# Row variances of layer norm moved from VectorE to GpSimd, with a rebuilt instruction order

## The chip, the cores and the metric

One core of one Trainium2 chip in each run. The metric is the device time of one execution in microseconds (us). All runs quoted here are in the fast state (granted TensorE clock 0.99 to 1.00), apart from one run of the kernel before that came in the slow state and is left out of every ratio.

## The reference, cut to what matters

Four residual layers over 2048 tokens of 512 values, alternating a linear attention (A) and a dilated local attention (B). A layer norm without learned parameters stands before each:

```python
def _layernorm(x, axis=-1, eps=1e-5):
    m = jnp.mean(x, axis=axis, keepdims=True)
    v = jnp.var(x, axis=axis, keepdims=True)
    return (x - m) / jnp.sqrt(v + eps)

x = A_x
x = x + _A_ref(_layernorm(x), A_wqkv, A_w_phi, A_wo)
x = x + _B_ref(_layernorm(x), B_wqkv, B_wo)
x = x + _A_ref(_layernorm(x), A_wqkv, A_w_phi, A_wo)
x = x + _B_ref(_layernorm(x), B_wqkv, B_wo)
# ... (the two attentions: softmax feature maps with running sums; 8 keys at distance 2)
```

## The kernel before

The tokens are worked on in four blocks of 512 (128 rows by 4 columns of row statistics). Three of the four norms get their statistics from the layer that comes before: the residual add leaves the row sums, a square on ScalarE leaves the sums of squares, and a small step `var` makes the variance from both. That is 3 norms x 4 blocks = 12 variances.

```python
def sq(t):                                   # ScalarE, four per block
    sqd = self.t2([D], "sqd")
    nc.scalar.activation(out=sqd[:], in_=xb[:, t, :], func=ACT.Square, accum_out=T["ss"][:, t:t + 1])

def var(lo, n):                              # VectorE: q = ss - u*u/D
    u = T["sums"][:, lo:lo + n]
    nc.vector.scalar_tensor_tensor(out=T["q"][:, lo:lo + n], in0=u, scalar=-1.0 / D, in1=u,
                                   op0=ALU.mult, op1=ALU.mult)
    nc.vector.tensor_tensor(out=T["q"][:, lo:lo + n], in0=T["q"][:, lo:lo + n],
                            in1=T["ss"][:, lo:lo + n], op=ALU.add)
# ... s_norm:
def ln():                                    # ScalarE: "the logarithm"
    nc.scalar.activation(out=U["lnv"][:, 0:n], in_=T["var"](), func=ACT.Ln, bias=self.eps_t[:, 0:1], scale=scale)
    nc.scalar.activation(out=U["rstd"][:, 0:n], in_=U["lnv"][:, 0:n], func=ACT.Exp, scale=-0.5)
def nmr():                                   # VectorE: -mean * rstd
    # ...
```

The program is a set of threads of steps. A list of thread numbers says in which order the steps are emitted, a string says which of two engines does each copy, and another string says which numbered buffer each new tile gets:

```python
for w in _ORDER.split():
    key = self.names[int(w, 36)]
    i = n.get(key, 0); n[key] = i + 1
    self.threads[key][i]()
# ...
def slot(self, kind):
    k = self.ntile[kind]; self.ntile[kind] = k + 1
    return kind + _SLOTS[kind][k]
```

Each engine works through its own instructions in emission order, so one that has to wait for another engine's result holds up the work behind it in the list.

Of the kernel before, what the change touches and what calls it, by code (L numbers as in the profile page):

```python
# [8 lines left out]
BF16 = mybir.dt.bfloat16  # L9
# [7 lines left out]
P = 128  # L17
# [24 lines left out]
    "half_k": ((0, 3), (1, 3)),  # L42
    "half_ln": (),
    "split": ((1, 2), (1, 3)),
    "v_dram": (),
    "half_mo": (),
    "rho_pad": 0,
# [10 lines left out]
av 8 i i i i i i i i i i i i 0 f 0 g e 2t 0 bs 9 h a d c 0 j k t i i j l 27 o p 3 3 d6 b 1x 1x t 1y o m 2 2 1q  # L58
1z 1x 1x q u t r 1q v x w n s 1r w 1s 4 20 y 21 1x 22 1x 23 1q 1q 1q 1q 1v 1w z 3d 3d 3d 1u 1t 25 3e 3e 3e z 5
3e 3e z z 26 10 18 18 d5 1 z 16 11 4i 15 6 1h 13 3d 3e 3e 25 25 26 18 25 18 12 26 26 28 26 26 26 26 19 12 28  # L60
2a 28 1h 18 14 12 12 1a 28 1c 3e 2g 2g 1f 2h 2h 1h 1h 1b 1i 2b 1b 1e 1d 29 2j 2k 1h 1j 1n 2r 1b 1l 2s 1b 2c 2r
1k 2s 17 2g 2g 2h 2h 1k 1k 2h 2h 2h 2h 2d 1g 2d 2d 2d 2e 2j 1m 35 36 32 2o 2o 33 2s 33 32 33 33 2r 2s 2s 1o 2o
2o 2d 2r 3a 1k 3a 1p 2p 2o 24 24 2s 24 2u 2v 35 37 2u 2u 2u 2s 2i 2w 2j 3a 2s 3a 2l 2z 2j 24 32 32 34 2m 3b 33
3d 3f 3f 2z 2z 2z 33 2f 33 33 2f 2f 2f 3a 3a 2q 2q 2q 30 3a 2n 3a 3a 2z 3e 2q 2x 35 35 b6 3b 3a 2y 31 31 31 31
3c 3c 38 3c 39 3c 3m 3f 3n 3o 3o 3o 24 24 3g 3g 3g 3f 3p 3q 3g 3g 3g 3g 3g 3r 3q 3f 3g 24 3h 3i 3i 5l 5m 5n 3p
3s 3q 3j 3k 3k 3t 3q 3p 3x 5m 3w 3u 3h 3i 3i 3q 3v 3q 3q 3y 3h 3i 3q 3i 3h 3i 3q 5l 5o 5p 5r 5m 5q 7 7 3z 3q
3i 3j 3k 5m 5l 5s 3k 7 7 5m 5m 5m 3h 3i 7g 40 5u 44 41 42 5t 5m 5m 3j 3j 7h 7i 3k 5v 5m 5w 43 7h 45 7j 45 60
3k 3k 3k 46 45 45 5y 5x 5z 61 61 48 47 47 61 49 47 4a 47 4b 62 47 4b 63 3j 4g 94 4c 45 4d 45 4e 4f 3k 45 45 61
64 63 4h 4p 65 95 7j 7j 66 4q 63 96 95 97 97 63 67 7h 63 67 69 7h 6b 4k 4k 4k 4l 4p 4r 4k 4m 4p 4p 4s 4t 7k 7n
6a 68 6c 4o 7m 50 50 4u 4u 4u 4n 4u 7l 4w 97 7o 7p 7p 7q 7s 3l 4x 7r 7r 7p 7t 7p 6o 7u 50 7r 7r 7v 6o 6j 4v 4y  # L70
4j 6o 6q 6o 4j 4z 6k 6p 6r 6j 7r 6e 6l 95 6d 95 7v 6t 6s 6f 6d 7w 6e 7z 7x 98 9b 9a 99 6g 7y 9c 6e 6j 6j 9d 9d
6u 9d 6e 6n 80 6m 9d 6h 6v 6v 9e 9h 9f 6i 9g 9f 6w 6v 6v 6w 6w 9f 9i 9f 87 88 8h 9j 9f 50 82 9j 9l 6w 6x 6x 87
87 6w 81 83 9n 6x 9k 87 8b 89 51 51 51 51 52 52 8c 8c 8e 6u 6u 6u 9m 8j 8a 8d 8c 6v 6y 3l 8f 82 9o 82 85 82 50
51 52 4z 4z 4z 9q 9q 9s 8c 6z 8g 6y 6z 9r 71 70 6y 6y 6z 6z 72 86 a0 a0 a1 73 84 8i 74 75 74 74 50 74 8i 76 8i
77 a2 76 79 53 53 54 55 54 a5 56 53 54 9v 78 76 9q 9q 76 a0 81 53 9v 9w 9p 7a 57 9v 9u a7 76 7a 9t 8j 7c 9y 54
58 59 59 59 9v 59 9x 7d 7e 5a 8j 8j 7b 7f 5c 5b 5d 5b 5b a0 8k 5e 5b 5f 8k 9z a7 5b 5f 5j 8k 8k 8l a3 5i b4 a4
b7 5h b4 b4 b4 8l 5g b5 b5 a7 b5 b5 a7 8k 8l 8j c3 8i c3 b8 c4 c4 c4 c4 a8 8m a8 a8 a8 c3 a9 a9 5k at c1 b5 a6
8m au au c1 c2 b5 c2 aw c2 c2 a8 a9 b5 b5 8n 8o 8n 8p 8m at au at at 8n 8q 8m a7 aa 8n aw 8r 8s au au au 8s 8s
8t au au 8s 8v a6 a6 8u aa 8w aa 8x 8u 8u 8u 8y ab ac ab ad a6 aa b7 8u b9 b7 c3 8y 90 92 c1 91 c1 c2 8z c2 c2
aw ay ab c2 ba ae ab af aw b0 c4 c4 b1 bc ag ag ag ag ah bc aj ak bc c1 c4 c4 bc al ax c3 ai ai ai bd b1 ai am  # L80
93 bf bi bg az bf ai am ar bf bf bg bg aq b7 bg bg bg bg bg bb an ao ag ag ap bi ag ag b1 b1 bc b2 c2 bi bn bi
bl bk as bq br br bq br br bq bq b1 br by by by by bt b3 b3 b3 b3 br be be be br br bz c5 c5 bh bj bn bn bn c5
bu c4 by by by by c6 bo by c6 c6 c5 bt bt bt bn bv c6 c6 c6 bz be bp bp bw bm bp bp c0 c0 by c6 c6 bx c0 c0 c9
c5 ca c6 cb cb cc cb cd ce cd fr fs c7 c8 c7 c8 c8 ft cc ci cf cd cg cd c7 c8 c8 fs fu c8 e2 fu ch cd e3 cd cc
cj ck e4 cd c7 c8 c8 c7 e3 e2 cm cd c8 e6 e7 fu cl cd cd cn cp co e5 e3 hb e3 cr e2 ea e9 cq hc cs e3 cs e8 e3
e3 hd eb ec e3 e3 e3 ed ct cv hc eh cs he ee cs ef cw eg ei cx ei ei cu ei cu cu cu fs cy fs fv ej cu cy d0 cz
ek d2 fw fx fz d3 cs cs fy cs cs g0 g0 g0 el ek em ek en ek d4 d1 dc g1 eo ek g2 g3 g2 dc de eo es g0 g4 dd dh
g2 g5 g2 he hc eq g6 d7 d8 d7 d7 d7 he di dc g2 dc d9 ep er hc et dn hf da db df dh dh dh hi hh hj hg hk hk hk
dj dk dl dm dm g6 g7 g9 dn dn dg ga f0 f0 hl hm hn hm ho hm ev ew f1 hk dn g8 do do hp f2 fa fc hm hq do do dp
ev ex fc gb ev f0 dp ey dn f3 f0 hm fc f4 hq ev ez fc do dp dn dq dq d6 f5 f6 dm dm eu hs gi gj gi fd gs hr fd  # L90
ht fd hu hv fd dq fe fe f5 f5 f8 f5 f9 f7 fb gk fd fe fc gn gn gp gi gi gl gm gd gd gd ge ic gf i7 i7 i9 gg i8
dr dr dt ds dr du hx hy gd dq gu dr dv gn gq gh i7 ff ia gu fb go ff fg fh fb fb eu gv gc gn i2 gr i3 hx hz hx
i7 i2 ib gv i4 hx i1 gc hw i2 i2 i5 gu i0 gu gv gv gw gt ie fg fi if i6 ie id gw if dw dx id gv gw id id ie ie
if if ig dw ff ig if ig fg fj dw e0 dw ff fg fk ie fl fm fl fn gu fl fl fp ih ih ih ih e1 ii ii ii ik ij fq dy
gt gt gt fo fo il io io io io ii im ip iq ip is ir ir ih ii in ip ip iu it ir gx ir gy gx gx gx gz gy h0 dz dz
iv gy h1 h4 gx gy h2 h4 iw iv h5 h5 h6 h7 gy h4 h3 h5 h8 h9 h7 h7 h4 h5 ha h7
# [4 lines left out]
    "0011111111111001110111111010000010010000000000000001011111101100100000110101000110000010000001110111"  # L101
    "1101011110010000110101000000000000001101011000000000100100000000000000000101111100000011011000000000"
    "0000000000001101111010000000100101011111010000011001110111000000000000000111111011101110010100101000"
    "00000000000001111001000000000000000000000000000000000000000000000000000000000001111"
# [5 lines left out]
        "0123456701231231456204632073205712053720457604356704213560421356720415763215063506432506"  # L110
    ),
    "med": (
        "0123456789abcdef5837ae98eeaeae471853bc9e43cbe47199ce3185413cebf94c8f74e3581bc71931bc7f370bf9ac21584e"
        "af9c37214a0b589dec37"
    ),
    "t2": (
        "0123450123450342150132451032451032451032451302153421530421503452014520345123045130425123504321504321"
        "5043215043210451023134"
    ),
    "ps": (  # L120
        "0123456701234750613250746132074365462150743510635127035164051362731405263710452763210743562107423251"
        "0764376215043762435107625407152367423167052341760543210675432170652147053624036542076314257603415203"
        "6415026734107534105234065265346053460562036207346201542015471204712603712035764120356471032516407324"
        "6735012463754021637261350247613025476130746513072463501742635017463015276301562703152760432764327014"
        "6570324650324705613245076"
# [4 lines left out]
class _Fast:  # L130
# [162 lines left out]
    def setup(self):  # L293
# [12 lines left out]
        self.VD = {}  # L306
# [202 lines left out]
    def s_out(self, st, key, b, Wo, last):  # L509
# [36 lines left out]
        def var(lo, n):  # L546
            if "q" not in T:
                T["q"] = self.sm([4], "q")
            u = T["sums"][:, lo:lo + n]
            nc.vector.scalar_tensor_tensor(out=T["q"][:, lo:lo + n], in0=u, scalar=-1.0 / D, in1=u,  # L550
                                           op0=ALU.mult, op1=ALU.mult)
            nc.vector.tensor_tensor(out=T["q"][:, lo:lo + n], in0=T["q"][:, lo:lo + n],
                                    in1=T["ss"][:, lo:lo + n], op=ALU.add)

        def norm(lo, n):
            add(st, "DVE", var, lo, n)
            V = {"var": lambda: T["q"][:, lo:lo + n], "sum": lambda: T["sums"][:, lo:lo + n]}
            self.s_norm(st, key, b, V, tuple(range(lo, lo + n)), 1.0 / D, 1.0 / D)
# [24 lines left out]
    def s_a1(self, L, b):  # L583
# [3 lines left out]
        G = 2 * H  # L587

# [48 lines left out]
        def t1(t, m):  # L637
            T["s1"] = self.sm([4 * G], "s1", F32, 1)
            nc.vector.tensor_tensor(out=T["s1"][:, 0:m * G], in0=T["s2"][:, 0:m * G, 0], in1=T["s2"][:, 0:m * G, 1],
                                    op=ALU.add)  # L640
# [36 lines left out]
        for t in range(4):  # L677
            add(st + "v", "PE", mv, t)
            self.flex(st + "v", ev, t)
        m = 2 if (L, b) in _OPT["half_k"] else 4  # L680
        for t in range(0, 4, m):
            for f in (t8, t4, t2, t1):
                add(st, "DVE", f, t, m)
# [235 lines left out]
    def s_b1(self, L, b):  # L919
# [83 lines left out]
        if (L, b) in _OPT["v_dram"]:  # L1003
            add(st + "v", "SP", vwr)
# [813 lines left out]
```

## Time and profile before

| | before |
|---|---|
| median, lowest to highest of the first runs | 330.5 us, 329.39 to 330.88 |
| span of the profiled run | 327.5 us |
| TensorE, VectorE, ScalarE, GpSimd busy | 310.3, 302.2, 279.3, 25.3 us |
| ScalarE's waits for the variance before the logarithm | 1.9 us in 7 waits |

The busy rows are sums over stages with different limits.

### The profile page before, as it was taken

The numbers are of one execution on the slowest core, as the hardware profiler recorded it, in microseconds if no ns is written. First come the engines' busy times: TensorE is split into PE (matmuls) and PEld (weight loads), VectorE is DVE, ScalarE is ACT, GpSimd is POOL, SyncE is SP. The second block draws the span as 40 slices with busy tenths as digits, with TensorE's granted clock in tenths as the row PEclk, the third lists the DMA queues.
The fourth block names the chain that finished last, engine by engine and source line by source line (L and its number), as shares of the span: only waits on it lengthen the run. The fifth ranks groups of instructions, "written<-read, shape, count | busy, mean of one in ns | idle before, by whom it ended". The sixth has DMA issues, their size and how long they took to land. (4 is left out here: it accounts for less than half of the span.)

```text
span 327.5 us, 8033 instructions
## 1 busy us (share of the span) xinstructions
PE 310.3 (95%) x3176; PEld 149.5 (46%) x3203; DVE 302.2 (92%) x439; ACT 279.3 (85%) x634; POOL 25.3 (8%) x50
## 2 busy tenths in 40 slices
PE   7999999999999999999999999979999999999873
PEld 3655456445444444443444455644544454433221
DVE  7998995998998999899999999699999999999993
ACT  5999988998888999989999999798999996676550
POOL 4000000000021003000000000000000208400000
PEclk9999999999999999999999999999999999999999
DMA  7980000004556899998750300023436977679952
GB/s 197 380 197 3 0 2 4 2 20 120 105 148 135 152 164 133 139 121 154 137 135 1 67 3 2 4 59 90 128 58 125 179 146 134 150 139 158 166 176 92
DMA packets 37388, 35.41 MB, mean 108 GB/s; under 512 B 23008, under 2 KB 32224, under 8 KB 37344
## 3 DMA queue, kind: packets, MB, share of 16 engines
q1 hardware_dynamic: 36816, 34.81, 53.6%
q8 instruction: 27, 0.44, 0.6%
q14 instruction: 17, 0.14, 0.2%
q10 hardware_dynamic: 528, 0.02, 0.1%
HBM read 10.50 MB, written 2.36 MB: 39 GB/s over the span
## 5 line engine op out<-in xcount | busy, mean ns | idle before, releaser
L927 PE MATMUL ps<-xnT,WB 128*128 128x512 bf16 x384 | 87.6, 380 | 0.5 <-DMA xnT<-xn 0.5
L1081 DVE TENSOR_TENSOR pav<-PT,Vg 128x4096 bf16<-128x4096 bf16 (+1 forms) x34 | 72.0, 2162 | 1.5 <-DMA Vg<-V 1.0
L1019 DVE TENSOR_TENSOR prod<-QT,K 128x4096 bf16<-128x4096 bf16 x32 | 72.5, 2291 | 0.3 <-ACT QT L192 0.2
L927 PEld LDWEIGHTS <-WB 128*128 128x128 bf16 x384 | 42.3, 114 | 43.3 <-issue 5.8
L520 PEld LDWEIGHTS <-oT 128*128 128x128 bf16 x256 | 23.8, 97 | 34.5 <-ACT oT L192 5.7
L192 ACT CAST oT<-ps 128x512 bf16<-128x512 f32 (+1 forms) x60 | 32.1, 587 | 8.4 <-PE ps L1090 7.1
L706 ACT ACTIVATE Eq<-ps 128x512 bf16<-128x512 f32 x64 | 34.0, 615 | 0.7 <-PE ps L698 0.6
L520 PE MATMUL ps<-WoB,oT 128*128 128x512 bf16 x122 | 32.1, 380 | 2.4 <-ACT oT L192 2.0
L599 ACT ACTIVATE Ek<-ps 128x512 bf16<-128x512 f32 x64 | 33.6, 622 | 0.4 <-PE ps L593 0.2
L698 PE MATMUL ps<-xnT,WA 128*128 128x512 bf16 x128 | 30.7, 380 | 0.6 <-DVE Eq L816 0.6
L540 ACT ACTIVATE sqd<-x 128x512 bf16<-128x512 bf16 x48 | 30.1, 643 | 1.0 <-DVE x L533 0.8
L605 PE MATMUL ps<-WA,xnT 128*128 128x512 bf16 x120 | 30.0, 380 | 0.5 <-issue 0.2
L593 PE MATMUL ps<-WA,xnT 128*128 128x512 bf16 x124 | 29.7, 380 | 0.6 <-DMA xnT<-xn 0.2
L520 PE MATMUL ps<-WoA,oT 128*128 128x512 bf16 x120 | 29.2, 380 | 0.4
L533 DVE SCALAR_TENSOR_TENSOR x<-ps,x 128x512 bf16<-128x512 f32 x38 | 25.4, 686 | 1.9 <-PE ps L520 1.7
L192 ACT CAST V<-ps 128x512 bf16<-128x512 f32 x31 | 17.5, 595 | 4.4 <-PE ps L927 4.3
L192 ACT CAST K<-ps 128x512 bf16<-128x512 f32 x31 | 17.8, 585 | 3.7 <-PE ps L927 3.3
L530 ACT ACTIVATE x<-ps 128x512 bf16<-128x512 f32 x26 | 15.1, 598 | 6.4 <-PE ps L523 6.3
L192 ACT CAST QT<-ps 128x512 bf16<-128x512 f32 x29 | 17.1, 592 | 2.5 <-PE ps L927 2.5
L651 DVE TENSOR_TENSOR Ek<-Ek,rk 128x4096 bf16<-128x4096 bf16 (+1 forms) x10 | 18.6, 1858 | 0.5 <-ACT rk L646 0.5
L593 PEld LDWEIGHTS <-xnT 128*128 128x128 bf16 x128 | 12.1, 97 | 15.4 <-DMA xnT<-xn 0.7
L446 ACT ACTIVATE xn<-x,nmr,rstd 128x512 bf16<-128x512 bf16 x23 | 18.2, 822 | 1.0 <-DVE nmr L435 0.8
(129 smaller groups left out, 433.3 us busy)
## 6 DMA issues: line engine op xcount, KB each, us to landing
Vg<-V SPq DMA_DIRECT2D x128, 131.5 KB, 4.4
Prho<-rd SPq DMA_DIRECT2D x8, 512.0 KB
x<-in_A_x_dram SPq DMA_DIRECT2D x3, 512.0 KB
WB<-in_B_wqkv_dram SPq DMA_DIRECT2D x3, 512.0 KB, 11.6
wraw<-in_A_wqkv_dram SPq DMA_DIRECT2D x4, 256.0 KB, 4.5
out_dram<-x SPq DMA_DIRECT2D x4, 256.0 KB, 2.2
out_dram<-x SPq DMA_DIRECT2D x8, 128.0 KB, 2.2
x<-in_A_x_dram SPq DMA_DIRECT2D x4, 128.0 KB
```

The lines of the kernel that those rows point to most:

```text
L192: self.nc.scalar.copy(out=out, in_=in_)
L520: nc.tensor.matmul(y[:], lhsT=oT[:, c, t * P:(t + 1) * P], rhs=Wo()[:, c, :], start=(c == 0), stop=(c == NB - 1 and not onpe))
L533: nc.vector.scalar_tensor_tensor(out=xb[:, t, :], in0=T[t][:], scalar=1.0, in1=xb[:, t, :], op0=ALU.mult, op1=ALU.add, **kw)
L540: nc.scalar.activation(out=sqd[:], in_=xb[:, t, :], func=ACT.Square, accum_out=T["ss"][:, t:t + 1])
L593: nc.tensor.matmul(pk[:], lhsT=xnT[:, t, k, :], rhs=self.WA[:, k, D:2 * D], start=(k == 0), stop=(k == NB - 1))
L599: nc.scalar.activation(out=T["E"][:, t, s, :], in_=T["k", t][:], func=ACT.Exp, scale=1.0 - 2.0 * s)
L605: nc.tensor.matmul(pv[:], lhsT=xnT[:, t, k, :], rhs=self.WA[:, k, 2 * D:3 * D], start=(k == 0), stop=(k == NB - 1))
L698: nc.tensor.matmul(pq[:], lhsT=self.WA[:, k, hb * P:(hb + 1) * P], rhs=xnT[:, :, k, :], start=(k == 0), stop=(k == NB - 1))
L706: nc.scalar.activation(out=self.Eq[L, b][s][:, :, hb, :], in_=T[hb][:].rearrange("p (t i) -> p t i", t=4), func=ACT.Exp, scale=1.0 - 2.0 * s)
L927: nc.tensor.matmul(pp[:], lhsT=self.WB[:, k, i * D + c:(i + 1) * D:NB], rhs=xnT[:, :, k, :], start=(k == 0), stop=(k == NB - 1))
L1019: nc.vector.tensor_tensor(out=pr[:], in0=QT[:, c:c + 1, :].to_broadcast([P, NW, TB]), in1=win, op=ALU.mult)
L1081: nc.vector.tensor_tensor(out=pv, in0=PT[:, :, lo:lo + n].unsqueeze(1).to_broadcast([P, NB, 2, n]), in1=vw, op=ALU.mult)
```

## The change

The intent: relieve VectorE, which is 92% busy, of a small job that GpSimd, 8% busy, can do; and, with a search that knows this, build a new order. The search was run with assumed rates of 85 GB/s for a broadcast and 130 GB/s for the copies of the values; these figures are not in the kernel, only their result is.

```diff
-    "half_k": ((0, 3), (1, 3)),
+    "half_k": {(0, 3): 1, (1, 3): 1},
+    "pool": ('var',),
 ...
 _ORDER = """        (all lines replaced; so are _CHOICE and _SLOTS)
 ...
         def var(lo, n):
-            u = T["sums"][:, lo:lo + n]
-            nc.vector.scalar_tensor_tensor(out=T["q"][:, lo:lo + n], in0=u, scalar=-1.0 / D, in1=u, ...)
-            nc.vector.tensor_tensor(out=T["q"][:, lo:lo + n], in0=T["q"][:, lo:lo + n], ...)
+            u, ss, q = (T[k][:, lo:lo + n] for k in ("sums", "ss", "q"))
+            if "var" in _OPT["pool"]:
+                T["qw"] = self.sm([4], "qw")
+                w = T["qw"][:, lo:lo + n]
+                nc.gpsimd.tensor_tensor(out=w, in0=u, in1=u, op=ALU.mult)
+                nc.gpsimd.tensor_scalar(out=q, in0=ss, scalar1=float(D), scalar2=None, op0=ALU.mult)
+                nc.gpsimd.tensor_tensor(out=q, in0=q, in1=w, op=ALU.subtract)
 ...
-            add(st, "DVE", var, lo, n)
+            add(st, "POOL" if "var" in _OPT["pool"] else "DVE", var, lo, n)
 ... (cut: the scale of the logarithm becomes 1/D^2; options that are not switched on)
```

## The prediction

> **What bounds the kernel now.** I read the page first (busy shares, then the slices), then a table of four stretches, the waits of VectorE, the groups of instructions that the change names, and the timeline of GpSimd.
>
> ```profile
> span 327.5 us, 8033 instructions
> PE 310.3 (95%) x3176; PEld 149.5 (46%) x3203; DVE 302.2 (92%) x439; ACT 279.3 (85%) x634; POOL 25.3 (8%) x50
> ```
>
> TensorE and VectorE are both almost full; ScalarE has about 48 us to spare and GpSimd nearly everything. An average over the span does not say who sets the end, so I cut the span at the second key-value transposition (at 209 us every block of the second linear layer has to meet there) and at the end of the last product of attention weights and values (319 us).
>
> ```profile
> core 0: us, PE busy (x) PEld busy (x) DVE busy (x) ACT busy (x) POOL busy (x), PEclk, DMA share, GB/s
> 0.00:58.00 58.00, 55.84 (x708) 31.08 (x714) 49.95 (x112) 51.03 (x108) 5.12 (x30) 1.00 0.38 110
> 58.00:209.00 151.00, 148.41 (x1476) 70.44 (x1488) 143.06 (x195) 140.23 (x327) 7.27 (x11) 1.00 0.55 94
> 209.00:319.00 110.00, 102.87 (x977) 46.93 (x984) 106.14 (x126) 87.62 (x200) 12.91 (x9) 1.00 0.65 126
> 319.00:327.50 8.50, 3.16 (x21) 1.03 (x19) 3.04 (x7) 0.42 (x2) 0.00 (x0) 0.94 0.30 101
> ```
>
> The reader is to see that the bound changes. Up to 209 us TensorE is busy 204.3 of 209 us, so 4.7 us at most can come out there by filling its gaps. From 209 to 319 us VectorE is busy 106.1 of 110 us (3.9 us idle) and TensorE less. The last 8.5 us are a fixed chain: last product, matmul, copy, output projection, residual, store. Gaps that a better order could fill are therefore 4.7 + 3.9 = 8.6 us, if nothing else changed.
>
> ```profile
> DVE q L552 <- ACT sqd L540: 1.1, 2, 0.8
> DVE pav L1081 <- DMA Vg<-V: 1.0, 1, 1.0
> ACT lnv L428 <- DVE q L552: 1.9, 7, 0.4
> ```
>
> (Waiter, what ended the wait, us in total, times, longest.) VectorE lost 1.1 us waiting for the sums of squares that the variance needs, and 1.0 us, once, for a copy of the values. So neither thing that the change treats costs much now.
>
> ```profile
> L550 DVE SCALAR_TENSOR_TENSOR q<-sums 128x4 f32<-128x4 f32 x12 | 1.9, 159 | 0.0
> L552 DVE TENSOR_TENSOR q<-q,ss 128x4 f32<-128x4 f32 x12 | 2.0, 166 | 2.1 <-ACT sqd L540 1.1
> L444 DVE TENSOR_SCALAR xn<-x,rstd,nmr 128x512 bf16<-128x512 bf16 x41 | 14.9, 408 | 0.4
> L446 ACT ACTIVATE xn<-x,nmr,rstd 128x512 bf16<-128x512 bf16 x23 | 18.2, 822 | 1.0 <-DVE nmr L435 0.8
> ```
>
> The two variance instructions are 1.9 + 2.0 = 3.9 us of VectorE in all. The last two rows are the same normalization on the two engines: 14.9/41 = 0.36 us on VectorE, 18.2/23 = 0.79 us on ScalarE.
>
> ```profile
> 249.17 0.24 POOL L953 COPY K<-K 128x64 bf16<-128x64 bf16 x1 [65.42 <-DVE x L533]
> 249.34 0.23 POOL L969 COPY vh<-V 128x64 bf16<-128x64 bf16 x1
> ...
> 270.79 2.24 POOL L953 COPY K<-K 128x64 bf16<-128x64 bf16 x1 [10.27 <-ACT K L192]
> 272.97 2.30 POOL L969 COPY vh<-V 128x64 bf16<-128x64 bf16 x1
> 275.33 2.18 POOL L965 COPY V<-vh 128x64 bf16<-128x64 bf16 x1
> ```
>
> ```profile
> 270.65 2.28 DVE L1081 TENSOR_TENSOR pav<-PT,Vg 128x4096 bf16<-128x4096 bf16 x1
> 272.85 2.32 DVE L1019 TENSOR_TENSOR prod<-QT,K 128x4096 bf16<-128x4096 bf16 x1
> 275.10 2.32 DVE L1081 TENSOR_TENSOR pav<-PT,Vg 128x4096 bf16<-128x4096 bf16 x1
> ```
>
> The same small copies take 0.24 us at 249 us, where VectorE adds residuals out of PSUM, and 2.2 to 2.3 us at 270 us, where each ends about 0.1 us after one long VectorE product (270.65 + 2.28 = 272.93; 270.79 + 2.24 = 273.03). GpSimd gets through one instruction per long VectorE product. VectorE pays little: 2.32 instead of 2.28 us, 0.04 us each time.
>
> **What the Trainium skill says.** "SBUF — State Buffer", § Who interferes with whom: a VectorE instruction with two SBUF inputs contends with a GpSimd instruction that reads SBUF, the later one waiting until the first is through, and one with at most one SBUF input does not. The trace agrees: 2.24 against 0.24 us above. "GPSIMD Engine Reference", § 3 Performance versus the Vector engine: two-input elementwise work is about twice as slow on GpSimd; for 4 columns that hardly matters, and no arithmetic of GpSimd is in this trace to check it. "Perfetto Trace Analysis", § GPSIMD Engine Instruction: a GpSimd span is not to be trusted, its spacing is; here the spacing (270.79, 272.97, 275.33) says 2.2 to 2.4 us as well. The same page, § Optimizing Scalar/DVE Operations, warns that moving work between VectorE and GpSimd might not help for this reason.
>
> **The change, part by part.**
> 1. *Variances.* Removed from VectorE: 12 x (0.159 + 0.166) = 3.9 us. Added to GpSimd: 12 x 3 dependent instructions. Beside residuals or copies out of PSUM I take 0.24 us each from the quiet copies, 0.7 us per variance. Beside long products the first can finish early (it needs the sums only), the other two come after the last sum of squares: 2 x 2.2 = 4.4 us, up to 6.6 us if all three are late. In the new order about half of the 12 stand beside two long products (first layer: three of four in the linear blocks and two in the local ones; second layer: the last). Cost to VectorE if every one of the 36 delayed it: 36 x 0.04 = 1.4 us; for half, 0.7 us.
> 2. *Who does what.* The string of choices is new too; I counted both built programs. VectorE gets +9 normalizations (9 x 0.36 = 3.3), +7 net PSUM copies of 128x512 (+4 keys, +3 outputs, +2 values, -1 query, -1 kv: 7 x 0.69 = 4.8), -1 transposed copy (-0.7), -3 residuals (3 x (0.69 + 0.08) = -2.3) and one product less out of PSUM (-0.3): +4.8 us. With the 3.9 us removed, VectorE has **+0.9 us**. So the freed time is spent at once. ScalarE gets -9 normalizations (-7.1), -7 net of those copies plus one extra of another kind and a transposed one (-2.6), +3 residuals (+2.4): **-7.3 us**. TensorE adds 3 identity matmuls for those residuals, 3 x 0.22 = **+0.7 us**.
> 3. *The order.* Adding the mean duration of each VectorE instruction listed after the second transposition gives 117.2 us before and 117.3 us after (durations overlap, the trace shows 109.2 busy us for these). So where VectorE sets the end there is no less for it to do. Before that point TensorE's sum is 216.4 and 216.2 us: also the same. What changes is the tail. At the last projection matmul of the second local layer the old list has 6 query-key products, 10 value products and 2 weight products left for VectorE, the new one 4, 10 and 2, that is 4.6 us less behind it. TensorE is fed later and should sit idle less from 290 us on, but VectorE's own queue is not shorter.
> 4. *The assumed transfer rates.* The copies from 267 to 308 us are 48 x 131.5 KB in 40.5 us, 156 GB/s. 130 GB/s is more cautious, so I expect no late values; worth 1.0 us. In the new tail the last two copies for block 2 wait until TensorE has read the first product of block 3; counting the products between, they have some 2 us of slack.
>
> Sum: of the 8.6 us of gaps I grant a third, -3 us, because a search made the new order and ScalarE is 7 us lighter, so TensorE's waits for copies out of PSUM (2.0 us on the output projection alone) should shrink; against it +0.7 us for VectorE's delays by GpSimd and about nothing for the +0.9 us, most of which lies before 209 us where VectorE has 16 us idle. Net -2.3 us: 330.5 - 2.3 = **328.2 us**.
>
> **Rivals.**
> - *ScalarE waits for the late variance.* The logarithm of the variance stands in ScalarE's queue 0 to 1.2 us of work behind the last square, and a variance beside long products takes 4.4 us. Some 6 such waits of up to 3 us would hold back the copies out of PSUM, and TensorE with them. For it: ScalarE was up to 99% busy in slices between 130 and 190 us. Against it: the old order already left 2 to 3 us there in places and the scheduler may know GpSimd's delay. If so, +1 to +4 us: 331 to 334 us.
> - *The freed VectorE time counts in full.* If the end followed VectorE's removed 3.9 us plus its 1.1 us of waiting for squares, 325.5 us. Against it: the total of VectorE is not smaller.
> - *The tail's copies come late.* If the 2 us of slack are not there, VectorE stands still before the last products, directly at the end: +1 to +3 us.
>
> **Range and chances.** 325 to 332 us. A gain over 2% (below 323.9 us) needs 6.6 of the 8.6 us of gaps: 5%. A loss over 2% (above 337.1 us) needs the first and third rival together: 4%. Within 2%: 91%.
>
> **What would show it.** Right: VectorE busy within 2 us of 303, ScalarE near 272, 12 x 3 GpSimd instructions of which about half take 2 us or more, the stretch from the second transposition to the last product still about 108 to 110 us with VectorE 97% busy, no wait of VectorE for values over 1 us. Wrong: a row of ScalarE waits for the variance above 5 us (first rival), VectorE busy well under 300 us (second), or VectorE waiting for values after 300 us (third).

## More of the kernel before

A pair of squares over the query and key weights feeds a flag that is checked at the end; their output is thrown away, but it needs a buffer, and takes it from the pool of 16 medium buffers that queries, keys and normalized rows use too:

```python
def sq(qk):                                  # s_bound, ScalarE, twice
    junk = self.med([NB, D], "sq")
    nc.scalar.activation(out=junk[:], in_=self.WA[:, :, qk * D:(qk + 1) * D], func=ACT.Square,
                         accum_out=self.okc[:, qk:qk + 1])
```

## The result, and the profile after

The new kernel took **344.72 us** (median; 342.85 to 346.25 in 4 runs) where the kernel before took 329.96 us (329.39 to 330.88, 4 runs): ratio 1.0442, 95% interval 1.0381 to 1.0502. It is slower by 14.8 us, where a gain of 2.3 us had been predicted. (A ratio is the mean time of one kernel's fast runs over the mean of the other's fast runs of the same rounds, so it is not quite the ratio of the medians.) The four runs spread over 3.4 us: the profiled one, at a granted clock of 0.999, took 342.85 us, the three at 0.987 to 0.989 took 344.35 to 346.25 us. A difference from this kernel's median, 344.72 us, is therefore uncertain by some 2 us (an estimate: the half-width of the interval, 0.6%).

The head of the new kernel's page:

```profile
span 341.1 us, 8046 instructions
PE 313.8 (92%) x3181; PEld 150.5 (44%) x3206; DVE 303.8 (89%) x424; ACT 273.4 (80%) x626; POOL 69.5 (20%) x86
```

The work is what was foreseen: VectorE 303.8 us, ScalarE 273.4 us. TensorE's busy time is 3.5 us more than before. Only GpSimd is busy longer by more than the loss (69.5 instead of 25.3 us): the 36 variance instructions take 26.6 us, and the same 18 small copies 37.5 instead of 19.8 us, mostly because standing behind VectorE's products counts as busy there. For the other engines the loss is idle time. The four stretches of the prediction, cut at the same two events (the second key-value transposition, now at 220 us instead of 209, and the end of the last value product, now at 332.5 instead of 319):

```profile
core 0: us, PE busy (x) PEld busy (x) DVE busy (x) ACT busy (x) POOL busy (x), PEclk, DMA share, GB/s
0.00:58.00 58.00, 55.23 (x691) 31.02 (x696) 50.11 (x112) 49.14 (x102) 5.57 (x31) 1.00 0.42 110
58.00:220.00 162.00, 152.19 (x1493) 71.62 (x1504) 143.98 (x185) 137.67 (x323) 38.32 (x34) 1.00 0.50 88
220.00:332.50 112.50, 103.26 (x981) 46.73 (x990) 106.45 (x118) 86.04 (x201) 25.65 (x21) 1.00 0.66 126
332.50:341.10 8.60, 3.11 (x22) 1.12 (x20) 3.23 (x12) 0.55 (x2) 0.00 (x0) 0.98 0.22 71
```

Eleven microseconds are lost before the transposition (162.0 instead of 151.0 us) and 2.5 after it. In the second stretch TensorE's idle time rose from 151.00 - 148.41 = 2.6 to 162.00 - 152.19 = 9.8 us, VectorE's from 7.9 to 18.0 us. The tail is the same. Next, the waits (waiter, what ended the wait, us in total, times, longest):

```profile
ACT lnv L426 <- POOL q L553: 13.9, 9, 2.8
DVE nmr L433 <- ACT rstd L429: 8.5, 9, 1.2
...
DVE QT L189 <- ACT sq L411: 4.3, 1, 4.3
...
DVE E L1041 <- ACT E L1037: 2.1, 1, 2.1
```

ScalarE stands 13.9 us for the variance (before: 1.9), and VectorE 8.5 us for what ScalarE makes of it (before: 0.3). A new wait of 4.3 us is that of a query copy for the weight squares. One of the variances in time (start, duration, engine, line, operation; in brackets the idle time before it and what ended it), block 3 of the first linear layer:

```profile
118.10 0.68 DVE L531 SCALAR_TENSOR_TENSOR x<-ps,x 128x512 bf16<-128x512 f32 x1
...
118.82 0.63 ACT L538 ACTIVATE sqd<-x 128x512 bf16<-128x512 bf16 x1 [0.17 <-DVE x L531]
...
119.29 0.20 POOL L551 TENSOR_TENSOR qw<-sums 128x4 f32<-128x4 f32 x1 [0.68 <-DVE x L531]
...
119.42 2.29 DVE L1085 TENSOR_TENSOR pav<-PT,Vg 128x4096 bf16<-128x4096 bf16 x1
119.62 2.17 POOL L552 TENSOR_SCALAR q<-ss 128x4 f32<-128x4 f32 x1
121.88 0.20 POOL L553 TENSOR_TENSOR q<-q,qw 128x4 f32<-128x4 f32 x1
122.11 0.30 ACT L426 ACTIVATE lnv<-q,eps_t 128x4 f32<-128x4 f32 x1 [2.58 <-POOL q L553]
...
123.83 0.18 DVE L1041 TENSOR_TENSOR E<-E,maskE 128x32 bf16<-128x32 bf16 x1 [2.12 <-ACT E L1037]
...
124.06 0.59 PE L1046 MATMUL ps<-E,indDen 128*128 128x512 bf16 x2 [1.48 <-DVE E L1041]
```

Read it downwards: the last square ends at 119.5, GpSimd's second instruction gets through when VectorE's product at 119.42 ends, so the variance is ready 2.5 us after the square. The list has put the logarithm right behind it, so ScalarE idles 2.58 us. The exponentials of an attention stand behind the logarithm, so VectorE, which needs one of them, idles 2.12 us, and TensorE 1.48 us behind VectorE. One late value of 128x4 stops three engines in turn.

How late the variance can be is seen from the two instructions that come after the last square (durations in ns: shortest, median, longest):

```profile
L552 POOL TENSOR_SCALAR q<-ss x12: 217/444/2259, 76.1 to 267.6; 128x4 f32<-128x4 f32 x12
L553 POOL TENSOR_TENSOR q<-q,qw x12: 200/200/202, 76.4 to 269.6; 128x4 f32<-128x4 f32 x12
```

In the new kernel only the first of the two is ever held up. The other took 0.20 us in all twelve variances: whenever it came, VectorE was idle or was reading PSUM. The same place in the kernel before:

```profile
109.96 0.63 ACT L540 ACTIVATE sqd<-x 128x512 bf16<-128x512 bf16 x1
...
110.69 0.58 ACT L192 CAST K<-ps 128x512 bf16<-128x512 f32 x1
...
111.38 0.17 DVE L552 TENSOR_TENSOR q<-q,ss 128x4 f32<-128x4 f32 x1
111.46 2.28 DVE L1019 TENSOR_TENSOR prod<-QT,K 128x4096 bf16<-128x4096 bf16 x1
111.58 0.30 ACT L428 ACTIVATE lnv<-q,eps_t 128x4 f32<-128x4 f32 x1 [0.31 <-DVE q L552]
```

There VectorE slips the variance in ahead of its next product, and ScalarE has a key copy to do meanwhile. Over all 12 variances, the old list puts 21 other ScalarE steps between the last square and the logarithm, the new list 12, counted in the two lists.

The other new wait, around the weight squares:

```profile
87.88 1.94 ACT L411 ACTIVATE sq<-WA 128x2048 bf16<-128x2048 bf16 x1
...
89.78 1.93 ACT L411 ACTIVATE sq<-WA 128x2048 bf16<-128x2048 bf16 x1
...
91.83 0.69 DVE L189 CAST QT<-ps 128x512 bf16<-128x512 f32 x1 [4.28 <-ACT sq L411]
92.56 2.29 DVE L1023 TENSOR_TENSOR prod<-QT,K 128x4096 bf16<-128x4096 bf16 x1
```

Both squares now stand together and hold ScalarE from 87.9 to 91.8 us. The second one's unused output lies in the buffer that the query copy gets next, so VectorE waits 4.28 us for rubbish to be written. In the kernel before, the squares are at 89.3 and 120.4 us, and only GpSimd waits for one of them, before a small copy; that wait is long, but old_order_short_squares below finds no cost.

```profile
POOL K L953 <- ACT sq L413: 13.6, 1, 13.6
```

The first query-key product of the local layer comes 7.4 us later than before (92.6 against 85.2).

### The profile page after: what moved, and what is told of

It reads as the page before. It is cut to its first block, busy times and chain, and to the rows that moved or that the text cites. A ratio compares the mean times of both kernels' runs of the same rounds, so it can differ in the third digit from the quotient of the medians.

```text
span 341.1 us, 8046 instructions
## 1 busy us (share of the span) xinstructions
PE 313.8 (92%) x3181; PEld 150.5 (44%) x3206; DVE 303.8 (89%) x424; ACT 273.4 (80%) x626; POOL 69.5 (20%) x86
## 4 chain that ended last, share of the span: by engine, by line
PE 23%; ACT 14%; DVE 13%; issue 10%; POOL 10%; DMA 7%; SPq 4%; DVEq 0%; POOLq 0%; ACTq 0%
PE ps L942 7%; DMA Vg<-V 6%; PE ps L518 5%; SPq L994 4%; DVE pav L1085 3%; POOL q L552 3%; DVE prod L1023 3%; ACT sqd L538 3%; POOL qw L551 3%; PE ps L610 2%; DVE x L531 2%; ACT oT L191 2%; PE ps L704 2%; DVE Eq L829 1%; POOL V L980 1%
## 5 line engine op out<-in xcount | busy, mean ns | idle before, releaser
L942 PE MATMUL ps<-xnT,WB 128*128 128x512 bf16 x384 | 87.9, 380 | 2.7 <-DVE x L531 1.8
L551 POOL TENSOR_TENSOR qw<-sums 128x4 f32<-128x4 f32 x12 | 11.5, 958 | 136.5 <-DVE x L531 132.5
L191 ACT CAST oT<-ps 128x512 bf16<-128x512 f32 (+1 forms) x57 | 30.9, 588 | 7.8 <-PE ps L1094 6.4
L518 PE MATMUL ps<-WoA,oT 128*128 128x512 bf16 x120 | 30.0, 379 | 1.3 <-DVE oT L189 0.9
L531 DVE SCALAR_TENSOR_TENSOR x<-ps,x 128x512 bf16<-128x512 f32 x35 | 23.0, 685 | 2.2 <-PE ps L518 1.4
L528 ACT ACTIVATE x<-ps 128x512 bf16<-128x512 f32 x29 | 17.1, 597 | 7.4 <-PE ps L521 7.3
L1094 PE MATMUL ps<-pav,indAV 128*32 128x512 bf16 (+1 forms) x272 | 18.2, 370 | 4.0 <-DVE pav L1085 3.8
L984 POOL COPY vh<-V 128x64 bf16<-128x64 bf16 x6 | 16.1, 2689 | 27.4 <-ACT V L191 27.4
```

What stands on the lines that cost most here:

```text
L191: self.nc.scalar.copy(out=out, in_=in_)
L518: nc.tensor.matmul(y[:], lhsT=oT[:, c, t * P:(t + 1) * P], rhs=Wo()[:, c, :], start=(c == 0), stop=(c == NB - 1 and not onpe))
L531: nc.vector.scalar_tensor_tensor(out=xb[:, t, :], in0=T[t][:], scalar=1.0, in1=xb[:, t, :], op0=ALU.mult, op1=ALU.add, **kw)
L942: nc.tensor.matmul(pp[:], lhsT=self.WB[:, k, i * D + c:(i + 1) * D:NB], rhs=xnT[:, :, k, :], start=(k == 0), stop=(k == NB - 1))
```

## The experiments

Fourteen runs, all with the right result (some are inexact, within the tolerance). In the tables of this section, "before" was measured in the same rounds and lay between 329.63 and 330.09 us. "Us won" counts from the new kernel's median, 344.72 us, and is uncertain by some 2 us, as said above. Where an edit changes what the variance is computed from, the scale of the logarithm is changed with it; that line is cut here.

### First call: whose loss is it, the engine's or the order's?

Theory when these were written: the late GpSimd variance makes the loss. Rival: the new order makes it, whoever computes the variance.

**var_dve_new_order**: the new order, `var` on VectorE at the same places of the list.

```diff
-            if "var" in _OPT["pool"]:
-                ... three gpsimd instructions
+            nc.vector.scalar_tensor_tensor(out=q, in0=u, scalar=-1.0 / D, in1=u, op0=ALU.mult, op1=ALU.mult)
+            nc.vector.tensor_tensor(out=q, in0=q, in1=ss, op=ALU.add)
```

> The new order unchanged, the variance computed by VectorE with the two old instructions at the very place in the list where GpSimd had it. Theory (the late result on GpSimd: three dependent instructions, each of which waits for a long VectorE product, holds up ScalarE's logarithm and with it everything that stands behind it): most of the 14.4 us comes back, 329 to 334 us, ScalarE's idle time before the logarithm under 4 us instead of 13.9. Rival (the new order itself, built for other transfer rates and choices, is the bad part): 340 to 345 us.

Measured: 342.64 us, ratio 1.0384 (1.0344 to 1.0424).

```profile
ACT lnv L426 <- DVE q L549: 6.8, 7, 2.7
...
DVE q L549 <- ACT sqd L538: 3.9, 6, 1.1
```

So taking GpSimd out gives back some 2 us, and even that is not clear: the interval and the new kernel's (1.0381 to 1.0502) overlap. I read this as "the order is the loss", which the second call showed to be too quick: at its place in the list, which did not matter to GpSimd, the variance now holds VectorE, which works in order, until the last square is done (3.9 us), and ScalarE still stands 6.8 us behind it. The new list is short of time at this hand-over, whoever makes it.

**var_pool_old_order**: the old order, the variance by the three GpSimd instructions.

```diff
-            nc.vector.scalar_tensor_tensor(...)
-            nc.vector.tensor_tensor(...)
+            nc.gpsimd.tensor_tensor(out=w, in0=u, in1=u, op=ALU.mult)
+            nc.gpsimd.tensor_scalar(out=q, in0=ss, scalar1=float(D), scalar2=None, op0=ALU.mult)
+            nc.gpsimd.tensor_tensor(out=q, in0=q, in1=w, op=ALU.subtract)
```

> The old order unchanged, its two VectorE instructions for the variance replaced by the three on GpSimd. Theory of the late result: slower by 6 to 14 us, 336 to 344 us, ScalarE idle before the logarithm 10 us or more. Rival (the new order is the bad part): 328 to 332 us.

Measured: 335.22 us, ratio 1.0162 (1.0122 to 1.0201).

```profile
ACT lnv L428 <- POOL q L555: 13.0, 9, 2.5
DVE nmr L435 <- ACT rstd L431: 9.3, 11, 1.3
```

GpSimd alone costs 5.2 us in an order made for VectorE, clear of noise, though 0.8 us less than the theory's lowest. The waits are as large as in the new kernel (13.0 and 9.3 us, against 13.9 and 8.5), but count for less: a sum of waits is not a price.

**var_dve_shadow_pool**: as var_dve_new_order, and GpSimd computes the same into tiles that nobody reads.

```diff
+            nc.gpsimd.tensor_tensor(out=w, in0=u, in1=u, op=ALU.mult)
+            nc.gpsimd.tensor_scalar(out=q2, in0=ss, scalar1=float(D), scalar2=None, op0=ALU.mult)
+            nc.gpsimd.tensor_tensor(out=q2, in0=q2, in1=w, op=ALU.subtract)
```

> As the first run, and GpSimd computes the variance too, into scratch tiles for which nobody waits. If what costs is the load that the 36 instructions put on GpSimd's queue[...] (halo copies and the copies of values then come late): near the kernel after, 338 to 345 us. If what costs is only the wait for the result: within 2 us of the first run.

Measured: 343.13 us, ratio 1.0392 (1.0341 to 1.0444), against 1.0384 without the shadow. The load that 36 GpSimd instructions put on VectorE costs nothing that these runs can tell (0.0008 of the ratio, where each interval is 0.004 to 0.005 wide to either side); what costs is waiting for their result.

**var_pool_one_late**: the new kernel with the factor 512 put into ScalarE's square, so that only one GpSimd instruction comes after the last square.

```diff
-            nc.scalar.activation(out=sqd[:], in_=xb[:, t, :], func=ACT.Square, accum_out=...)
+            nc.scalar.activation(out=sqd[:], in_=xb[:, t, :], func=ACT.Square, scale=float(D) ** 0.5, accum_out=...)
-                nc.gpsimd.tensor_scalar(out=q, in0=ss, scalar1=float(D), scalar2=None, op0=ALU.mult)
-                nc.gpsimd.tensor_tensor(out=q, in0=q, in1=w, op=ALU.subtract)
+                nc.gpsimd.tensor_tensor(out=q, in0=ss, in1=w, op=ALU.subtract)
```

> The new kernel, the factor 512 put into ScalarE's square, so that GpSimd has two instructions, and only one of them after the last square. Theory of the late result: about half of the loss comes back, 335 to 340 us, ScalarE idle before the logarithm 5 to 8 us. Rival (order): 342 to 346 us.

Measured: 340.91 us, ratio 1.0339 (1.0302 to 1.0376): 3.8 us less than the new kernel. The wait for the variance fell only from 13.9 to 11.3 us, since the one instruction left still has to get past a long VectorE product: five of the twelve took 1.9 to 2.1 us. What went is the short last one, 0.3 us from the end of the second to its own end in the timeline above. Both the time and the wait are short of what was expected (335 to 340 us, 5 to 8 us).

### Second call: no variance at all, and the weight squares

The first call could not say what the order costs by itself, as each engine for the variance brings its own waits. So: no variance. The logarithm takes the mean square alone, without the square of the mean; the result is slightly wrong.

**novar_new_order**, and **novar_old_order** as the same edit in the kernel before:

```diff
         def var(lo, n):
-            ... all instructions
+            return
-            V = {"var": lambda: T["q"][:, lo:lo + n], ...
+            V = {"var": lambda: T["ss"][:, lo:lo + n], ...
```

> New order with no variance instruction at all (the logarithm takes the mean square alone, so the result is slightly wrong on purpose). Theory A, the order itself is the loss: still about 340 us, ratio to the kernel before at least 1.03, since its stalls are not at the variances. Rival B, the new order is only sensitive to when the variance comes: under 334 us, ratio under 1.012.

> Old order with no variance instruction at all (slightly wrong result on purpose): the most that taking the variance off VectorE can gain. Theory A: VectorE's 3.9 us count only in part before the second transposition, 328 to 330 us. Rival B, VectorE sets the end: 326 us.

Measured: new order 333.16 us, ratio 1.0103 (1.0072 to 1.0135); old order 330.03 us, ratio 0.9999 (0.9979 to 1.0018). With the first call that makes a table (medians, us):

| variance by | VectorE | GpSimd | nobody |
|---|---|---|---|
| old order | 330.0 | 335.2 | 330.0 |
| new order | 342.6 | 344.7 | 333.2 |

Three things follow. In the old order the variance was free on VectorE: the whole of it taken away gains nothing (to within 0.7 us by the interval), so the change had nothing to win there. The new order by itself, with its other choices of engines and buffers, loses 3.1 us. And in the new order the variances together cost 11.5 us on GpSimd (344.7 - 333.2), and 9.5 us on VectorE at those places. The reading of the first call, that the order is the loss whatever is done about the variance, fell; it is an order that cannot bear a late variance.

**squares_own_slot**: the new kernel, two characters of the buffer string changed, so that the weight squares write to another medium buffer.

```diff
-        "...6f7cde86dec63463dce67f..."
+        "...6f7cde86deccc463dce67f..."
```

> New kernel, the two weight squares write their unused output to another medium buffer, one whose next writer comes late, so that the first query copy of the local layer and a broadcast no longer wait for them; ScalarE still does both squares there. Theory A1, that wait starts the delay of 7.4 us at the first query-key product: VectorE's 4.3 us wait is gone, time about 340 to 341 us (3 to 4 us less than the new kernel). Rival: ScalarE is held 3.9 us by the two squares anyway and TensorE waits for its copies instead: within 1 us of the new kernel's 344.7.

Measured: 342.32 us, ratio 1.0385 (1.0349 to 1.0422). VectorE's 4.3 us wait is gone. The median is 2.4 us lower, but this interval and the new kernel's (1.0381 to 1.0502) overlap. And ScalarE now waits 2.9 us for a transposition that still reads that buffer:

```profile
ACT sq L411 <- DMA xnT<-xn: 2.9, 1, 2.9
```

So this does not separate VectorE's wait from ScalarE's 3.9 us of squares cleanly: inconclusive on that.

**squares_short**: the new kernel, each square covers 128 columns of 2048 and writes to a small buffer of its own. The flag checks less, the output is the same.

```diff
-            junk = self.med([NB, D], "sq")
-            nc.scalar.activation(out=junk[:], in_=self.WA[:, :, qk * D:(qk + 1) * D], ...)
+            self.slot("med")                 # the number is used up, so that all others stay
+            if qk == 0:
+                self.sqj = self.const.tile([P, P], BF16, name="sqj")
+            nc.scalar.activation(out=self.sqj[:], in_=self.WA[:, 0, qk * D:qk * D + P], ...)
```

> New kernel, the two weight squares cover 128 of 2048 columns each and write to a buffer of their own, so that neither the wait nor ScalarE's 3.9 us at 88 us is left (the flag that they feed then checks less; the result is the same). Theory A1: 338 to 340 us, 1 to 2 us under the variant that takes away only the wait. Rival, the delay at 88 us is caught up by 209 us since other waits stand behind it: within 1.5 us of the new kernel's 344.7.

Measured: 338.96 us, ratio 1.0286 (1.0255 to 1.0317). The squares at 88 us cost the new kernel 5.8 us.

### Third call: where, and does it add up?

**log_later**: the new kernel with the logarithm one or two ScalarE steps later in seven of the twelve norms.

```diff
  _ORDER: seven tokens moved, e.g. block 3 of the first linear layer
- ... var  ln   exp  exp  copy ...
+ ... var  exp  exp  ln   copy ...
```

> New kernel with the logarithm of the variance put one or two ScalarE instructions later in seven of the twelve normalizations, nothing else. Theory C, the new list puts the logarithm straight behind the variance, so ScalarE stands still while GpSimd works: the sum of those waits falls from 13.9 to under 9 us and the time to 339 to 342 us. Rival, the normalization itself is what the rest waits for, so putting its logarithm later only moves the wait to VectorE: within 1.5 us of 344.7, or slower.

Measured: 341.32 us, ratio 1.0352 (1.0332 to 1.0372), 3.4 us won. ScalarE's wait fell from 13.9 to 10.1 us, a little less than expected, and VectorE's wait for the result rose from 8.5 to 12.3 us. So the theory holds for the time, and the rival for part of the mechanism: some of the wait only changes place. One of the seven logarithms stood before the weight squares, and VectorE's wait for these fell as well, from 4.3 to 2.5 us; how much of the 3.4 us that is worth was not tested.

```profile
DVE nmr L422 <- ACT rstd L418: 12.3, 11, 2.5
ACT lnv L415 <- POOL q L542: 10.1, 8, 1.8
DVE QT L178 <- ACT sq L400: 2.5, 1, 2.5
```

**novar_short_squares**: novar_new_order with the edit of squares_short.

> New order without any variance instruction (slightly wrong result on purpose) and with the two weight squares short and out of the shared buffer: what is left of the order's own loss of 3.1 us. Theory: the squares are most of it, 330 to 331.5 us. Rival, the loss is caught up behind them: within 1 us of 333.2.

Measured: 330.06 us, ratio 1.0020 (0.9999 to 1.0042). Without variances and with short squares the new order is as good as the old one, and no better. The squares are its own loss, to within the noise: 333.16 - 330.06 = 3.1 us, or 0.0083 of the ratio, 2.7 us. So the new choice of engines and buffers costs nothing else that these runs can tell.

**novar_in_four**: the new kernel without the variance in four norms only, blocks 2 and 3 of the first linear layer and blocks 1 and 0 of the first local layer.

```diff
+        none = st in ("a4_02o", "a4_03o", "b3_01o", "b3_00o")
         def var(lo, n):
+            if none:
+                return
```

> New kernel without the variance in four of the twelve normalizations only: blocks 2 and 3 of the first linear layer, blocks 1 and 0 of the first local layer (slightly wrong on purpose). In the traces these four carry 6.5 of the 9.9 us by which the new kernel falls behind the one without any variance. Theory: 337.5 to 339 us. Rival, every variance costs about the same, 11.5/12 us each: 341 us.

Measured: 336.64 us, ratio 1.0210 (1.0193 to 1.0228): 8.1 us won, by a third of the variances; more than expected (337.5 to 339 us).

```profile
ACT lnv L426 <- POOL q L557: 5.1, 5, 1.7
```

In the new kernel's trace ScalarE's idle times before these four logarithms are 1.53, 2.58 (shown above), 2.76 and 1.16 us:

```profile
101.03 0.30 ACT L426 ACTIVATE lnv<-q,eps_t 128x4 f32<-128x4 f32 x1 [1.53 <-POOL q L553]
...
145.29 0.30 ACT L426 ACTIVATE lnv<-q,eps_t 128x4 f32<-128x4 f32 x1 [2.76 <-POOL q L553]
...
157.66 0.30 ACT L426 ACTIVATE lnv<-q,eps_t 128x4 f32<-128x4 f32 x1 [1.16 <-POOL q L553]
```

They are 8.0 us together, and taking them away wins 8.1 us; with an uncertainty of some 2 us, so close an agreement is luck. The waits before the other eight add up to some 6 us and are worth 336.64 - 333.16 = 3.5 us.

**later_one_late_own_slot**: log_later, one late instruction and the other buffer, together.

> The mends together, result exact: logarithms later, one late GpSimd instruction instead of two (the factor 512 is in ScalarE's square), squares in another buffer. If the gains add (2.4 for the buffer, 3.8 for one late instruction, 3 to 5 for the logarithms): 333 to 336 us. Rival, they treat the same delay and overlap: 337 to 340 us. Neither beats the kernel before.

Measured: 341.15 us, ratio 1.0370 (1.0330 to 1.0409), no better than one late instruction alone. The profile says why, and it is a fault of the experiment:

```profile
ACT sq L400 <- DMA xnT<-xn: 6.4, 1, 6.4
```

Putting an early logarithm later made a transposition later, which reads the buffer that I had given to the squares; ScalarE stood 6.4 us. The run says nothing on whether the gains add.

### Fourth call: the combination mended, and a control

**later_one_late_short**: the same with short squares instead of the other buffer, and without moving that early logarithm.

> The mends together without the fault of the last combination (there the buffer given to the squares was still being read by a late transposition, and ScalarE stood 6.4 us): logarithms later in six normalizations, one late GpSimd instruction instead of two, squares short. If the gains add (5.7 for the squares, 3.8 and about 3 for the others): 332 to 334 us. Rival, they are on one chain and overlap: 336 to 339 us.

Measured: 334.82 us, ratio 1.0156 (1.0134 to 1.0178): 9.9 us won, of 5.8 + 3.8 + 3.4 = 13.0 for the three alone (the 3.4 with seven logarithms, here six). That lies between the two expectations: they add for the most part, not in full. What is left over the kernel before is 4.9 us, and ScalarE still waits 7.0 us for variances.

**old_order_short_squares**: the kernel before with the edit of squares_short.

> Kernel before with the two weight squares short and in a buffer of their own: the control for the squares, and the only candidate for beating the kernel before. Theory, in the old order nothing waits for them: within 0.5 us of the kernel before. Rival, 3 to 4 us of ScalarE between 89 and 123 us count: 327 to 328 us.

Measured: 329.74 us, ratio 1.0007 (0.9986 to 1.0029). In the old order the squares cost nothing. No version that ran beats the kernel before.

## Why the prediction was wrong

The prediction was 328.2 us, the range 325 to 332, and 4% for a loss over 2%. Two steps failed. ScalarE's wait for the late variance stood outside the sum, as a rival of +1 to +4 us; it measured 11.5 us. The new order stood in the sum with -3 us; it measured +3.1 us. By its own steps:

- *What bounds the kernel.* TensorE up to 209 us is borne out: the loss came there, as soon as TensorE was kept waiting. That VectorE sets the end from 209 to 319 us is not: without its variances (four of the twelve lie there, 4 x 0.325 = 1.3 us) the old order is no faster, 0.9999; from the start of the copy that feeds the second transposition to the end of the last product it takes 110.72 us with them and without them, while VectorE's busy time there falls from 106.14 to 105.26 us. In the new kernel that stretch took 112.5 us, not 108 to 110, with VectorE busy 106.45 / 112.5 = 95% of it, not 97%.
- *Variances.* The work was right: VectorE's busy time is 303.8 us where about 303 was given. The delay on GpSimd was there, though less often than said: 8 of the 36 instructions took over 2 us, where it was to be half of them; all 36 sum to 26.6 us. And the two products after the last square, 2 x 2.2 us, did not happen: the third instruction took 0.20 us each time. VectorE's own delay, +0.7 us in the sum, is too small for the shadow run to show.
- *Who does what.* Right: ScalarE is busy 273.4 us where about 272 was given. One reading was wrong: the identity matmuls of the residuals are 128x512 and take 0.38 us each in both traces, so three more are 1.1 us, not 0.7; 0.22 us is that of the 128x128 transpositions.
- *The order, and the sum: the first step that failed.* "Of the 8.6 us of gaps I grant a third, -3 us, because a search made the new order and ScalarE is 7 us lighter." Nothing in the profile carried that; it was trust in the search. The order without variances and squares measured 330.06 us, so without the squares this term is 0, and with them +3.1. I had the placement and the buffers of the squares in the two lists, compared only totals and the tail, and never asked which new neighbours share a buffer.
- *The first rival, left out of the sum: the second step that failed, and the larger; its mechanism was right, its size wrong.* It said that ScalarE would wait for the late variance, "some 6 such waits of up to 3 us", and made of this +1 to +4 us. The trace has 9 waits, the longest 2.8 us, 13.9 us together (its own sign for this was a row above 5 us), and they are worth 11.5 us. So it needed no second rival for a loss over 2%: 11.5 us are 3.5%. The discount had two grounds. One was that the old order leaves 2 to 3 us there in places: true of the old list (21 steps), but the new one leaves less (12). The other was that most of it would be hidden: the four waits in the middle of the first two layers were hardly hidden, 8.0 us of waiting for 8.1 us of time.
- *Assumed transfer rates and the tail.* Right in what it denied: from 300 us on each product of weights and values starts 13.9 us later than before, the last one 13.5 us, so the third rival did not happen. Whether the assumed rates led the search to its tight places cannot be told from the kernel and stays open.
- *The second rival*, freed VectorE time that counts in full, is refuted by novar_old_order.

As measured, 330.0 + 3.1 for the squares + 11.5 for the late variances = 344.6 us, against 344.7. That it closes proves nothing, as both terms are differences along one path from the one kernel to the other. Along the other path the squares go first: they are worth 5.8 us, and the variances 338.96 - 330.06 = 8.9 us. So some 3 us of the loss need both, and belong to neither alone.

## What to carry to other kernels

Before moving a small job to an idle engine, take the job out altogether: here that run would have shown that there was nothing to win, for the cost of one wrong result. Then look at who waits for the job's result and how many instructions stand between; the answer's delay counts, not the work, and a value of 128x4 can stop three engines one after another. A new order from a search is to be checked for new waits on shared buffers and for the distance from each producer to its consumer, not by its totals.

## What the Trainium skill lacked or had wrong

- "SBUF — State Buffer", § Who interferes with whom, has the rule (a two-input VectorE instruction and a GpSimd read exclude each other) and it held: a variance instruction of 128x4 took 0.20 us in quiet and up to 2.26 us beside a product. What it lacks is the consequence for a chain. Beside VectorE products without a gap GpSimd gets through about one instruction per product (2.11 and 2.26 us one after the other at 140.6 us), so one instruction after the last input is enough to be late: leaving out the other took only 3.8 of 344.7 us. Nor does that section say which engine goes next after a wait: two GpSimd copies of 128x64 in the new kernel's trace took 4.71 and 7.97 us, longer than one product of 2.3 us.
- "GPSIMD Engine Reference", § 3 Performance versus the Vector engine, compares throughput (about twice as slow on large tiles). For 128x4 the quiet durations are close, 0.20 against 0.16 us; nothing there warns that the delay to the consumer decides, 11.5 us here.
- "Perfetto Trace Analysis", § Optimizing Scalar/DVE Operations, warns that a move between VectorE and GpSimd might not help. Here it harmed, and GpSimd's load on VectorE was not the reason: a shadow of the same 36 instructions left the ratio at 1.0392 against 1.0384.
